# Router products of the values: weights stationary in three column groups, result copied and transposed back

## The chip, the cores and the metric

The kernel runs on one core of a Trainium2 chip. The metric is device time in microseconds (us), the median of three runs. Engines are named as in the profile: PE is TensorE, DVE is VectorE, ACT is ScalarE, POOL is GpSimd, SP is SyncE.

## What is computed

An attention layer with hash buckets (2 batches, 8 heads, 768 tokens, 64 columns a head), a mixture of 8 experts with one expert per token, and a dense layer of two matrices. The change lies in the first two: the router's logits are the attention's output times the gate's weights. The kernel does not form them from the finished output. It multiplies the values with the gate's weights first and lets these products pass through the attention as 8 more columns of each head.

```python
def _attn_ref(q, k, v, proj):
    ...
    mask = q_bucket[:, :, :, None] == k_bucket[:, :, None, :]
    scores = np.where(mask, scale * np.matmul(q, k.transpose(0, 1, 3, 2)), -1000000000.0)
    ...
    return np.matmul(attn, v)

def _moe_ref(x, w_gate, w1, w2, capacity):
    logits = x @ w_gate
    expert_idx = np.argmax(logits, axis=1)
    ...
```

## The kernel before

The order of the work is written out by hand. The attention runs as 96 steps, 16 heads with 6 blocks of keys each (`for k in range(STEPS + LAG + 2)`, line 810). In each step PE gets `scores` of block k (two halves, lines 442 and 443, into two buffers `ps_t`), `mx` of a block 8 steps ahead (two matmuls, line 425, into three buffers `ps_m`), and in every odd step `pv` of two blocks (lines 470 to 472). ACT takes the exponential (444) and makes the high half (452), POOL makes the low half (`plo`, 458), DVE takes the maxima of `mx` (428). Everything else is put on the engines' queues at given moments: `due(x)` (lines 811 and 829) is called at the start of a step (k - 0.5, ahead of `scores`) and at its end (k), and issues whatever `spread` has made due by then; each `yield` of a generator lets d steps pass.

`vgate(r)` (line 522) serves one pair of heads. It is called 8 times; they are called product 0 to product 7 here. Its third part multiplies the pair's values, which lie transposed in `vt` (128 x 768), with the gate's weights `w` (128 x 16: 8 columns for each head of the pair, zero in the other head's rows): six matmuls with 128 columns of `vt` stationary and the 16 columns of `w` moving. The fourth and fifth parts, one for each head, split the result on DVE into a high and a low half in `vh` (lines 540 and 541, called the split here). For products 2 to 7 the parts come one step apart (`vgd`), the third at the start of step 12 r - 2. Product 1 starts at 7.75 (`vg0`), so its third part comes at the end of step 10; product 0 is at steps 2 to 4.

The result lies in `misc`, a pool of a single PSUM bank (`ps_x`, line 312) that six users share in turn. Whoever takes it next can write only when the last reader of the tile before is done. The users that follow a product are `bits` (line 389: `psb`, the projections of four heads, 4 matmuls of 128 x 32 stationary and 384 moving columns into 32 partitions each, two such tiles, then DVE's line 387) and `vscale` (line 558: the maximum `am` on DVE, line 563, is transposed on PE into `psn`, line 571). `vscale(1)` starts at step 13.25 and its transposition stands at the start of step 15; for `vscale(2)` this is the start of step 39, behind product 3; for `vscale(3)` step 63, behind product 5. `bits(2)` comes at the end of step 26, behind product 2, `bits(3)` at the end of step 50, behind product 4.

On DVE's queue there are besides `lo` of a head's preparation (line 375), the low half of the values (line 679) and the maxima of the raw values (line 554).

Of the kernel before, what the change touches and what calls it, by code (L numbers as in the profile page):

```python
# [9 lines left out]
F32 = mybir.dt.float32  # L10
# [9 lines left out]
P = 128  # L20
# [3 lines left out]
NC = S // P  # L24
# [3 lines left out]
KD = DM // P  # L28
E = 8
# [34 lines left out]
def moe_attention_kernel(ctx, tc, qk, v, vt, pj, wg, w1, w2, win, wout, out, cap):  # L64
    nc = tc.nc
    pe, act, dve, pool, sp = nc.tensor, nc.scalar, nc.vector, nc.gpsimd, nc.sync
# [3 lines left out]
    def opened(stack, name, bufs, side="left", **kw):  # L70
        return stack.enter_context(tc.tile_pool(name=name, bufs=bufs, side=side, reuse_waits="tile", **kw))
# [11 lines left out]
    def persist(shape, dt, name):  # L83
        return const.tile(shape, dt, tag=name, name=name)

    xd = dram.tile([NT + 1, DM], F32, tag="xd", name="xd")
    ident = persist([P, P], F32, "ident")
# [6 lines left out]
    iota_s = persist([P, NS], F32, "iota_s")  # L94
    tokid = persist([P, NS], F32, "tokid")
    rank8 = persist([P, E], F32, "rank8")
    wg_sb = persist([P, KD, 2, E], F32, "wg_sb")
    isw = persist([P, 1], F32, "isw")
    lg = persist([P, B, NC, E], F32, "lg")
    ids = persist([P, E, NW], I32, "ids")  # L100
# [84 lines left out]
    def bc(a, n):  # L185
        return a.unsqueeze(len(a.shape)).to_broadcast(list(a.shape) + [n])

    def mid(a, n):
        return a.unsqueeze(1).to_broadcast([a.shape[0], n] + list(a.shape[1:]))
# [114 lines left out]
    with ExitStack() as actx:  # L304
        pa = opened(actx, "pa", 1)
        pr = opened(actx, "pr", 6)
        ph = opened(actx, "ph", 1)
# [35 lines left out]
        def misc(name):  # L343
            return ps_x.tile([P, 512], F32, tag="x", name=name)
# [177 lines left out]
        def vgate(r):  # L522

            sw = sw_t[r // 2]
            t = vt_t.pop(r)
            yield
            yield
            ps = misc(f"psg{r}")
            w = wg_sb[:, r % KD].rearrange("p h e -> p (h e)")
            for j in range(NC):  # L530
                pe.matmul(  # L531
                    ps[:, j * 2 * E : (j + 1) * 2 * E], t[:, j * P : (j + 1) * P], w, start=True, stop=True
                )
            yield
            ps = ps[:, 0 : NC * 2 * E].rearrange("p (c h e) -> p c h e", h=2, e=E)
            for hh in range(2):
                h = 2 * r + hh
                t = vh(h)
                o, ol = hh * D, VA + hh * D
                dve.tensor_scalar(out=t[:, :, o : o + E], in0=ps[:, :, hh], scalar1=sw, scalar2=None, op0=ALU.mult)  # L540
                dve.scalar_tensor_tensor(
                    out=t[:, :, ol : ol + E], in0=ps[:, :, hh], scalar=sw, in1=t[:, :, o : o + E],
                    op0=ALU.mult, op1=ALU.subtract,
                )
                yield
# [68 lines left out]
        def unmatched(r):  # L614

            b, k = divmod(r, KD)
            rows = xd[1 + b * S : 1 + (b + 1) * S, k * P : (k + 1) * P].rearrange("(p c) d -> p c d", c=NC)
            n = 2 * NC * D
            vt = pr.tile([P, S], F32, tag="r", name=f"uv{r}").rearrange("p (h c d) -> p h c d", h=2, c=NC)
            sp.dma_start(out=vt.rearrange("p h c d -> p (h c d)"), in_=v[:, r * n : (r + 1) * n])  # L620
            last = r == NH // 2 - 1
            if not last:
                x = pr.tile([P, S], F32, tag="r", name=f"ux{r}").rearrange("p (c d) -> p c d", c=NC)
                sp.dma_start(out=x, in_=rows)
            m = pt.tile([P, S], F32, tag="pf", name=f"um{r}", bufs=4)
            ps = misc(f"psu{r}")
            for c in range(NC):
                pe.matmul(ps[:, 0:P], ones, vt[:, :, c], start=c == 0, stop=c == NC - 1)
            act.activation(m[:, 0:P], ps[:, 0:P], AF.Copy, scale=1.0 / S)
            ps = misc(f"psc{r}")  # L630
            pe.transpose(ps[:, 0:P], m[:, 0:P], ident)
            act.activation(m[:, P : 2 * P], ps[:, 0:P], AF.Copy, scale=SW)
            ps = misc(f"psl{r}")
            pe.matmul(
                ps[:, 0 : 2 * E], m[:, P : 2 * P], wg_sb[:, k].rearrange("p h e -> p (h e)"), start=True, stop=True
            )
            z = nm[:, 2 * r : 2 * r + 2].rearrange("p h c -> p c h")
            y = pt.tile([P, S], F32, tag="pf", name=f"uy{r}", bufs=4).rearrange("p (c h d) -> p c h d", c=NC, h=2)
            dve.tensor_tensor(
                out=y, in0=bc(z, D), in1=mid(m[:, 0:P].rearrange("p (h d) -> p h d", h=2), NC), op=ALU.mult  # L640
            )
            if last:

                x = xp_t[r][:, :, E : E + D]
                dve.tensor_tensor(out=x, in0=x, in1=y[:, :, 0], op=ALU.add)
                x = pv_t[2 * r + 1][:, 0 : NC * VA].rearrange("p (c d) -> p c d", d=VA)
                t, n = y[:, :, 1], nm[:, 2 * r + 1]
                dve.tensor_scalar(
                    out=t, in0=t, scalar1=sc_t[r // 2][:, 0:1], scalar2=float(S), op0=ALU.mult, op1=ALU.mult
                )  # L650
                dve.tensor_tensor(out=x[:, :, 0:D], in0=x[:, :, 0:D], in1=t, op=ALU.add)
                dve.scalar_tensor_tensor(
                    out=x[:, :, DE], in0=n, scalar=float(S), in1=x[:, :, DE], op0=ALU.mult, op1=ALU.add
                )
            else:
                dve.tensor_tensor(out=x, in0=x, in1=y.rearrange("p c h d -> p c (h d)"), op=ALU.add)
                sp.dma_start(out=rows, in_=x)
            y = pt.tile([P, S], F32, tag="pf", name=f"uz{r}", bufs=4)[:, 0 : NC * 2 * E]
            y = y.rearrange("p (c h e) -> p c h e", c=NC, h=2)
            dve.tensor_tensor(  # L660
                out=y, in0=bc(z, E), in1=mid(ps[:, 0 : 2 * E].rearrange("p (h e) -> p h e", h=2), NC), op=ALU.mult
            )
            for hh in range(2):
                dve.tensor_tensor(out=lg[:, b], in0=lg[:, b], in1=y[:, :, hh], op=ALU.add)

        def vh(h):
            if h not in vh_t:
                vh_t[h] = pt.tile([P, NC, VW], F16, tag="vh", name=f"vh{h}", bufs=4)
            return vh_t[h]
# [34 lines left out]
        for n in range(2):  # L704
            for i, t in enumerate(("X", "K2")):
                c = slice(n * HS, (n + 1) * HS)
                ps = (ps_m, ps_t)[i].tile([P, 512], F32, tag="mt"[i], name=f"psf{n}{i}")
                pe.matmul(
                    ps[D : D + 12, :HS], pj_sb[i * D : (i + 1) * D, 12 * i : 12 * i + 12], r0[i * D : (i + 1) * D, c],
                    start=True, stop=True,  # L710
# [75 lines left out]
        for h in range(NH):  # L786
            k = NC * h + NC - 1 + LAG
            if h < NH - 1:
                at(k + Q["ev"], evac, h)
            if h % 2 == 0:  # L790
                if h == 0:
                    spread(Q["vg0"][0], vgate(0), Q["vg0"][1])
                else:
                    spread(Q["vg0"][2] if h == 2 else NC * h + Q["vg"][h % 4 // 2], vgate(h // 2), Q["vgd"])
            elif h < NH - 1:
                at(k + Q["pa"], pair, h // 2)
                at(NC * h + Q["lvt"], load_vt, h // 2 + 1)
# [35 lines left out]
        with tc.If(ru > 0):  # L833
            for r in range(NH // 2):
                rr = nc.values_load(nflag[0:1, r : r + 1], min_val=0, max_val=2 * S)
                with tc.If(rr > 0):
                    unmatched(r)
            run(route(0, lambda: misc("psr1")))
            run(weigh(0))
        h = NH - 1  # L840
# [633 lines left out]
```

## Time and profile before

| what | us |
|---|---|
| median of three runs | 677.04 (676.58 to 677.83) |
| the profiled execution | 675.88 |
| its span | 674.1 |
| PE busy | 638.4 (95%), 5518 instructions |
| DVE busy | 481.0 (71%), 1038 instructions |
| ACT busy | 426.6 (63%) |
| POOL busy | 229.8 (34%) |

The attention fills the span up to about 235 us, the experts follow to about 410, the dense layer to the end. A matmul's duration includes its way through the array, so matmuls overlap in time; what one adds is read from the distance of two starts. Times of a row are microseconds from the span's start, then the duration; a bracket at the end gives how long the engine stood idle before it and who ended that.

### The profile page before, as it was taken

The page shows a single profiled execution, that of the slowest core. Times are in us where ns is not written, and L with a number is a line of the kernel's source. Part 1 is how long each engine was busy: PE and PEld are TensorE (multiplying, and loading weights), DVE is VectorE, ACT ScalarE, POOL GpSimd, SP SyncE. Part 2 cuts the span into 40 slices and gives each one's busy share as a digit, 9 for nine tenths or more (in the row PEclk, how much of TensorE's full clock was granted, in tenths as well). Part 3 has the DMA queues.
Part 4 walks back from the last instruction along what each step waited for, and adds up shares of the span by engine and source line. Part 5 has one row for each costly group of instructions (what it writes and reads, how often), then busy time and mean ns, then how long its engine had stood idle before and what let it go on. Part 6 is the DMA issues. An engine that isn't in the chain of part 4 may idle for free.

```text
span 674.1 us, 14367 instructions
## 1 busy us (share of the span) xinstructions
PE 638.4 (95%) x5518; PEld 479.7 (71%) x5518; DVE 481.0 (71%) x1038; ACT 426.6 (63%) x869; POOL 229.8 (34%) x199
## 2 busy tenths in 40 slices
PE   7899999999999769999999999999999999999894
PEld 2588889989899638999999997555555555555541
DVE  6768898898999957888888877888888452222320
ACT  3467778778787826776667765455445576555730
POOL 4339769769778233221077500000000021000011
PEclk9889999999999978999999999999999999999998
DMA  8584764764465065777677735443442011000011
GB/s 236 127 233 115 231 177 122 233 169 109 126 160 165 25 217 193 250 246 257 213 253 228 243 115 162 137 145 126 150 134 92 0 48 48 1 0 1 1 41 59
DMA packets 37840, 94.14 MB, mean 140 GB/s; under 512 B 7576, under 2 KB 13720, under 8 KB 37760
## 3 DMA queue, kind: packets, MB, share of 16 engines
q1 hardware_dynamic: 34672, 85.71, 42.7%
q0 software_dynamic: 2400, 7.36, 3.2%
q8 instruction: 46, 0.75, 0.4%
q14 instruction: 34, 0.28, 0.1%
q10 hardware_dynamic: 688, 0.03, 0.1%
HBM read 67.14 MB, written 6.29 MB: 109 GB/s over the span
## 4 chain that ended last, share of the span: by engine, by line
PE 75%; DVE 10%; DMA 6%; ACT 5%; issue 2%; SPq 0%; POOL 0%; POOLq 0%; ACTq 0%; DVEq 0%
PE psg L1249 16%; PE pso L1276 15%; PE psh L1006 11%; PE psy L1033 11%; PE psm L425 5%; PE pst L442 4%; PE pst L443 3%; DVE mx L428 2%; DMA out_dram<-os,inv 2%; PE psv L470 2%; PE psv L471 2%; PE psv L472 2%; PE psg L531 2%; DMA vr<-in_v_dram 1%; ACT junk L1203 1%
## 5 line engine op out<-in xcount | busy, mean ns | idle before, releaser
L458 POOL TENSOR_TENSOR plo<-pf,phi 128x768 f16<-128x768 f32 x86 | 147.1, 1736 | 60.4 <-ACT phi L452 24.9
L444 ACT ACTIVATE pf<-pst 128x384 f32<-128x384 f32 x192 | 83.5, 486 | 47.4 <-PE pst L443 45.7
L428 DVE TENSOR_REDUCE mx<-psm 128x1 f32<-128x384 f32 x192 | 96.3, 548 | 20.0 <-PE psm L425 19.7
L1291 POOL DMA_INDIRECT out_dram<-os,inv x12 | 12.1, 1008 | 270.8 <-DVE os L1283 244.5
L163 DVE SCALAR_TENSOR_TENSOR wl<-raw,wh 128x1024 f16<-128x1024 f32 (+1 forms) x68 | 82.7, 1218 | 6.3 <-ACT wh L157 5.2
L1249 PE MATMUL psg<-yTh,ch 128*128 128x512 f16 (+1 forms) x256 | 83.4, 326 | 3.2 <-DVE rl L1252 3.2
L1249 PE MATMUL psg<-yTl,ch 128*128 128x512 f16 (+1 forms) x256 | 83.4, 326 | 0.0
L1249 PE MATMUL psg<-yTh,cl 128*128 128x512 f16 (+1 forms) x256 | 83.4, 326 | 0.0
L1252 DVE SCALAR_TENSOR_TENSOR rl<-rl,psg 128x512 f32<-128x512 f32 x64 | 35.0, 551 | 64.4 <-ACT rl L1251 64.0
L442 PE MATMUL pst<-Y,K 128*128 128x384 f32 x192 | 75.2, 392 | 2.0 <-ACT pf L444 2.0
L1249 PEld LDWEIGHTS <-ch 128*128 128x128 f16 x512 | 50.0, 98 | 35.9
L452 ACT ACTIVATE phi<-pf 128x768 f16<-128x768 f32 x85 | 71.7, 844 | 1.9
L1276 PE MATMUL pso<-ch,gh 128*128 128x512 f16 x192 | 72.8, 379 | 0.0
L1276 PE MATMUL pso<-ch,gl 128*128 128x512 f16 x192 | 72.8, 379 | 0.0
L1276 PE MATMUL pso<-cl,gh 128*128 128x512 f16 x192 | 72.8, 379 | 0.0
L425 PE MATMUL psm<-K,X 76*128 76x384 f32 x192 | 66.8, 431 | 4.6 <-DVE mx L428 3.8
L157 ACT ACTIVATE wh<-raw 128x1024 f16<-128x1024 f32 (+1 forms) x68 | 67.6, 999 | 0.5 <-issue 0.4
L1276 PEld LDWEIGHTS <-gh 128*128 128x128 f16 x384 | 37.6, 98 | 42.3
L443 PE MATMUL pst<-X,K 77*128 77x384 f32 x192 | 66.5, 346 | 0.0
L1033 PE MATMUL psy<-hh,wl 128*128 128x224 f16 x256 | 66.3, 259 | 0.0
L1033 PE MATMUL psy<-hh,wh 128*128 128x224 f16 x256 | 66.3, 259 | 0.0
L1033 PE MATMUL psy<-hl,wh 128*128 128x224 f16 x256 | 66.3, 259 | 0.0
(231 smaller groups left out, 1495.2 us busy)
## 6 DMA issues: line engine op xcount, KB each, us to landing
raw<-in_w_dram SPq DMA_DIRECT2D x64, 512.0 KB
rc<-in_win_dram SPq DMA_DIRECT2D x16, 512.0 KB
rc<-in_wout_dram SPq DMA_DIRECT2D x16, 512.0 KB
r<-in_qk_dram SPq DMA_DIRECT2D x16, 384.0 KB
K<-hi SPq DMA_DIRECT2D x31, 192.0 KB
vr<-in_v_dram SPq DMA_DIRECT2D x4, 768.0 KB
vt<-in_vt_dram SPq DMA_DIRECT2D x8, 384.0 KB
Y<-hi SPq DMA_DIRECT2D x16, 192.0 KB
```

The source lines that it names most:

```text
L163: dve.scalar_tensor_tensor(out=wl[e, i][:, c : c + n], in0=r, scalar=(S1, S2)[i // 2], in1=wh[e, i][:, c : c + n], op0=ALU.mult, op1=ALU.s ...
L425: pe.matmul(ps[:, :HS], st["X"][0:76, c::NC], st["K2"][0:76, n * HS : (n + 1) * HS], start=True, stop=True)
L428: dve.tensor_reduce(out=mm[:, c, n : n + 1], in_=ps[:, :HS], axis=AX.X, op=ALU.max)
L442: pe.matmul(ps[:, :HS], st["K1"][:, kc], st["Y"][:, qc], start=True, stop=False)
L443: pe.matmul(ps[:, :HS], st["K2"][0:77, kc], st["X"][0:77, qc], start=False, stop=True)
L444: act.activation(pf.rearrange("k (c n p) -> k c n p", c=NC, n=2)[:, :, n], ps[:, :HS].rearrange("k (p c) -> k c p", c=NC), AF.Exp, scale=0 ...
L452: act.activation(phi_t[k], pf_t[k], AF.Copy)
L458: eng.tensor_tensor(out=plo_t[k], in0=pf_t.pop(k), in1=phi_t[k], op=ALU.subtract)
L1006: pe.matmul(ps, l[:, c], r[:, k], start=n == 0, stop=n == 3 * KD - 1)
L1033: pe.matmul(ps, l, r, start=n == 0, stop=n == 3 * KF - 1)
L1249: pe.matmul(ps, l, x, start=n == 0, stop=n == 3 * KD - 1)
L1276: pe.matmul(po[blk][s], l, r, start=first and n == 0, stop=last and n == 2)
```

## The change

The weights get 32 columns (16 of them zeros) and become the stationary side; 256 columns of `vt` move. Three matmuls write 32 partitions each, so the result comes out transposed, 96 x 256, in columns 0 to 255 of the same PSUM tile. DVE copies it to SBUF (`gv`), and two transpositions on PE write it back, token by row, into columns 256 to 447 of the tile, where the split reads it. This makes two parts more: matmuls, copy, transpositions, split of the first head, split of the second head. Nothing else is moved, so both splits come two steps later than before. The clearing and the scaling of `wg_sb`, and its maximum, go over 128 columns where they went over 64.

```diff
-    wg_sb = persist([P, KD, 2, E], F32, "wg_sb")
+    wg_sb = persist([P, KD, 4, E], F32, "wg_sb")
...
             w = wg_sb[:, r % KD].rearrange("p h e -> p (h e)")
-            for j in range(NC):
+            for i in range(3):
                 pe.matmul(
-                    ps[:, j * 2 * E : (j + 1) * 2 * E], t[:, j * P : (j + 1) * P], w, start=True, stop=True
+                    ps[32 * i : 32 * i + 32, 0 : 2 * P], w, t[:, 2 * i * P : (2 * i + 2) * P], start=True, stop=True
                 )
             yield
-            ps = ps[:, 0 : NC * 2 * E].rearrange("p (c h e) -> p c h e", h=2, e=E)
+            gv = ph.tile([96, 2, P], F32, tag="gv", name=f"gv{r}")
+            dve.tensor_copy(gv, ps[0:96, 0 : 2 * P].rearrange("p (m k) -> p m k", m=2))
+            yield
+            ps = ps[:, 2 * P : 2 * P + 192]
+            for m in range(2):
+                pe.transpose(ps.rearrange("p (i m x) -> p m i x", i=3, m=2)[:, m], gv[:, m], ident[0:96, 0:96])
+            yield
+            ps = ps.rearrange("p (c h e) -> p c h e", h=4, e=E)
             for hh in range(2):
...
-                ps[:, 0 : 2 * E], m[:, P : 2 * P], wg_sb[:, k].rearrange("p h e -> p (h e)"), start=True, stop=True
+                ps[:, 0 : 2 * E], m[:, P : 2 * P], wg_sb[:, k, 0:2].rearrange("p h e -> p (h e)"), start=True, stop=True
```

The last edit lies in a branch for rows without a match.

## Rows read from the trace of the kernel before

**Rows 1.** The page: its head, and the chain's shares by engine
```profile
span 674.1 us, 14367 instructions
...
PE 75%; DVE 10%; DMA 6%; ACT 5%; issue 2%; SPq 0%; POOL 0%; POOLq 0%; ACTq 0%; DVEq 0%
```

**Rows 2.** Timeline of PE around product 2 (start, us, engine, line, out<-in)
```profile
76.67 1.48 PE L531 MATMUL psg<-wg_sb,vt 128*128 128x16 f32 x12
78.00 0.42 PE L442 MATMUL pst<-Y,K 128*128 128x384 f32 x1
```

**Rows 3.** Timeline of PE around a tile of bits behind pv
```profile
90.80 0.20 PE L472 MATMUL psv<-vh,plo 128*128 128x73 f16 x1
90.93 0.85 PE L398 MATMUL psb<-r,pj_sb 128*32 128x384 f32 x8
91.71 0.44 PE L442 MATMUL pst<-Y,K 128*128 128x384 f32 x1
```

**Rows 4.** Timeline of PE around four transpositions in the experts
```profile
272.92 0.60 PE L989 MATMUL psa<-ident,xg 128*128 128x128 f32 x4
273.35 0.26 PE L1033 MATMUL psy<-hh,wh 128*128 128x224 f16 x1
```

**Rows 5.** DVE's groups by form: line, op, shapes, count | busy, mean ns
```profile
L1252 DVE SCALAR_TENSOR_TENSOR rl<-rl,psg 128x256 f32<-128x256 f32 x32 | 13.4, 418 | 6.0 <-ACT rl L1251 5.7
```

**Rows 6.** Timeline of all engines where the second tile of bits takes the bank
```profile
50.27 0.85 PE L398 MATMUL psb<-r,pj_sb 128*32 128x384 f32 x8 [0.43 <-DVE b L387]
```

**Rows 7.** Timeline of DVE from step 12 to the maximum that vscale(1) transposes
```profile
57.47 1.02 DVE L428 TENSOR_REDUCE mx<-psm 128x1 f32<-128x384 f32 x2 [0.53 <-PE psm L425]
58.41 1.33 DVE L375 SCALAR_TENSOR_TENSOR lo<-r,hi 128x768 fp32r<-128x768 f32 x1
59.67 0.26 DVE L540 TENSOR_SCALAR vh<-psg,sw 128x48 f16<-128x48 f32 x1
...
60.15 1.01 DVE L428 TENSOR_REDUCE mx<-psm 128x1 f32<-128x384 f32 x2
61.07 0.54 DVE L554 TENSOR_REDUCE am<-vr 128x1 f32<-128x384 f32 x1
61.65 0.16 DVE L563 TENSOR_REDUCE am<-am 128x1 f32<-128x4 f32 x1
```

**Rows 8.** Timeline of PE: the transposition of vscale(1)
```profile
61.86 0.27 PE L571 MATMUL psn<-ident,am 128*1 128x128 f32 x1 [0.43 <-DVE am L563]
```

**Rows 9.** Timeline of DVE: line 375 with POOL idle
```profile
35.10 0.95 DVE L375 SCALAR_TENSOR_TENSOR lo<-r,hi 128x768 fp32r<-128x768 f32 x1
```

**Rows 10.** Timeline of POOL in three stretches
```profile
57.27 1.66 POOL L458 TENSOR_TENSOR plo<-pf,phi 128x768 f16<-128x768 f32 x1
...
84.93 1.65 POOL L458 TENSOR_TENSOR plo<-pf,phi 128x768 f16<-128x768 f32 x1
...
109.67 1.71 POOL L458 TENSOR_TENSOR plo<-pf,phi 128x768 f16<-128x768 f32 x1 [0.23 <-ACT phi L452]
```

**Rows 11.** Timeline of DVE ahead of the transposition of vscale(2)
```profile
111.20 1.00 DVE L375 SCALAR_TENSOR_TENSOR lo<-r,hi 128x768 fp32r<-128x768 f32 x1
...
112.59 1.01 DVE L428 TENSOR_REDUCE mx<-psm 128x1 f32<-128x384 f32 x2
113.52 0.14 DVE L563 TENSOR_REDUCE am<-am 128x1 f32<-128x4 f32 x1
```

**Rows 12.** Timeline of PE: the transposition of vscale(2)
```profile
113.76 0.27 PE L571 MATMUL psn<-ident,am 128*1 128x128 f32 x1
```

**Rows 13.** Timeline of DVE in step 25, behind product 2
```profile
85.83 1.57 DVE L375 SCALAR_TENSOR_TENSOR lo<-r,hi 128x768 fp32r<-128x768 f32 x1
```

**Rows 14.** Timeline of PE: PE waits in step 25, and the first tile of bits(2)
```profile
84.57 0.55 PE L425 MATMUL psm<-K,X 76*128 76x384 f32 x1 [0.33 <-DVE mx L428]
...
87.54 0.85 PE L398 MATMUL psb<-r,pj_sb 128*32 128x384 f32 x8
```

**Rows 15.** Table by stretch: stretch, us, PE busy (x), PEld, DVE, ACT, POOL, granted clock, DMA share, GB/s
```profile
26.83:30.24 3.41, 3.41 (x11) 1.93 (x9) 0.99 (x3) 1.82 (x3) 2.37 (x2) 0.51 1.02 214
```

## The prediction

> **What bounds the kernel now.** I read the page first: PE carries 75% of the chain that ended last, inside a span of 674.1 us [rows 1]. So a microsecond taken from PE in the attention is worth one at the end, as long as PE finds its next operands ready. The second view is PE's timeline around a product: between 40 and 235 us PE issues almost without a gap, and a product is a solid block in it [rows 2]. The third view is PE's few real waits. They are short, and nearly all end with something that DVE has finished: a maximum [rows 14], the maximum that `vscale` transposes [rows 8], the release of the `misc` bank [rows 6]. DVE is therefore the second bound, and the question is what the change puts ahead of those releases. The fourth view is DVE's timeline at these places [rows 7, 11, 13], next to POOL's [rows 10].
>
> **The change part by part.** *The matmuls.* Twelve passes hold PE from 76.67 to 78.00, 1.33 us [rows 2]. The new form stands in the trace with other sizes: four matmuls of 128 x 32 weights and 384 columns into four groups of partitions, eight passes, from 90.93 to 91.71, 0.78 us, 0.13 after the last `pv` matmul where 0.03 is usual [rows 3]. With 256 columns it lies between two thirds of this, 0.52, and all of it, 0.78. I take 0.57, near the lower end, because with 384 columns most of the time is the columns' own. The switch costs 0.10 more. PE saves 1.33 - 0.67 = 0.66 us at each product (0.45 to 0.71).
>
> *The transpositions.* Four of them go from 272.92 to 273.35, 0.11 each [rows 4]; two cost 0.22 (0.06 to 0.55: between passes that overlap wholly and two that follow each other at the 0.27 that one lasts [rows 12]). So PE alone would keep 0.44 at a product.
>
> *The copy.* The trace has no copy of 256 columns out of PSUM. The nearest row is an operation on 128 x 256 that reads PSUM, 0.42 us [rows 5]; the ends are the split's 0.26 for 48 columns [rows 7] and 0.55 for a maximum over 384. I take 0.42. The transposed way needs it ahead of the split, so DVE has 8 x 0.42 = 3.4 us more.
>
> *The order on DVE and the bank.* The split of one head takes DVE 0.48 us, from 59.67 to 60.15 [rows 7]. Both splits now come two steps later, and the bank stays taken until the second is done. The next user of the bank must wait for that, and PE works in order: behind the waiting instruction stand the scores, the maxima's matmuls and `pv`, and so ACT, POOL and DVE. That the bank is waited for is seen in rows 6: `bits` stands 0.43 us because line 387 has not yet read the tile before. In the kernel before, the products' own release was always long past. I go through the places.
>
> *Product 1, then vscale(1).* The matmuls save 0.66, so step 12's maxima start at about 56.8, not 57.47; the row shows that DVE waited 0.53 for PE there. Line 375 follows at 57.7. It takes 0.95 with POOL idle [rows 9] but 1.33 here, and ends at 59.74, 0.81 after POOL's operation of 57.27 + 1.66 = 58.93 [rows 7, 10]; at 84.93 + 1.65 and 109.67 + 1.71 the distance is 0.82 both times [rows 10, 11, 13]. So it waits for POOL's operation and ends at 59.74 again: DVE's lead is gone. After it came the second split, and in its place now only PE's transpositions. Then: maxima 59.67 to 60.60, first split to 61.08, lines 554 and 563 (0.65 from start to the next start) to 61.73, maxima of step 14 to 62.66, second split (0.48 and the 0.06 of its end) to 63.20, and 0.05 for the signal. The transposition of `vscale(1)` starts at 63.25 and not at 61.86 [rows 8]: +1.35 (rounded down; -0.4 if the bank's release hid behind something I overlook, +1.6 if the copy takes 0.55).
>
> *Products 3 and 5, then vscale(2) and vscale(3).* The pattern repeats 52 us later, so one stands for both. Here the splits stood ahead of line 375; now the first stands behind it, between line 554 and the maxima at 112.59, and the second behind line 563 at 113.52 [rows 11]. If line 375 ends at 112.20 as before, the maxima start at 113.07, line 563 at 114.0, the second split ends at 114.6, and the transposition starts at 114.7 where it was at 113.76 [rows 12]: +0.95. DVE reaches line 375 about 1.2 us sooner than at 111.20, near 110.0; POOL's operation began at 109.67 [rows 10], so it is 0.3 too late to pass ahead of it. If it does pass, 1.2 us come back: -0.2. I take +0.95.
>
> *Products 2 and 4, then bits.* The second split now follows line 375, which ends at 87.40 [rows 13], 0.82 after POOL's operation of 84.93 [rows 10]. It ends at 87.9, and `bits`, at 87.54 now [rows 14], starts at 87.95 or so: +0.4. But the splits no longer delay the maxima for which PE waits at 84.57 [rows 14] (0.33 of PE idle, 0.66 with the shortened overlap), and DVE arrives at line 375 at about 84.9, just when POOL's operation starts. If it goes first, nothing waits: -0.44 - 0.66 = -1.1. The ends are too close to call, so I take the middle, -0.4.
>
> *The rest.* Product 0 lies where PE waits for transfers and DVE; the copy lets line 375 at 35.10 [rows 9] start some 0.2 sooner, and the wider clearing, maximum and scaling of the weights cost less than 0.1 (64 columns more, against 0.42 for 256 [rows 5]): -0.2 (-0.4 to +0.3). Product 6: the copy stands behind line 679, which waits for POOL, and the transpositions wait for the copy; between -0.44 (nothing waits) and +0.6: I take +0.2. Product 7 is followed by the stretch without maxima, where DVE and ACT set the pace: 0 (-0.44 to +0.5).
>
> The sum: 1.35 + 2 x 0.95 - 2 x 0.4 - 0.2 + 0.2 + 0 = +2.45 us. Everything behind the attention moves along unchanged. The profiled execution has 675.88 us, its span and 1.8 around it; it would take 678.3. It lies 1.16 below the median of the runs, so the forecast for the median is 677.04 + 2.45 = 679.5 us.
>
> A page speaks to this change. The Trainium skill, page "TensorEngine Tiling (Array Packing)", section "Theoretical Speedup", gives up to four times for a dimension of at most 32; by it the product would take 0.33 and the change would save 8 x (1.33 - 0.33 - 0.22) = 6.2 us. The same page, section "PSUM Bottleneck", says that tiling speeds up TensorE but not the way out of PSUM, whose copy may become the bottleneck; by it the 8 copies of 0.42 would set the time, +3.4 us. Rows 3 show 0.78 us for four groups, which is no fourfold gain for this form, and of the second rule no row shows a case.
>
> **The rivals.** *The covers hold (faster).* If the bank is free when the next user comes, because DVE gets its lines 375 through ahead of POOL everywhere, PE keeps 7 x 0.44 = 3.1 us, and 2 x 0.6 from the wait of rows 14: 677.0 - 4 = 673 us. For it: DVE waits for PE in many places, 0.53 in rows 7. Against it: the second split is the last or the next to last thing on DVE's queue ahead of three transpositions. It decides at 0.4 us of slack per place.
>
> *The fourfold gain.* Three matmuls wholly side by side, at a third or a quarter of 1.33, with no wait for the bank: 671 us. Against it stand the 0.78 of rows 3. It is the case of the page's rule above.
>
> *Gains and waits cancel (no change).* If line 375 passes ahead of POOL at products 2 and 4, or at 3 and 5, but not at both, the sum is 2.45 - 1.4 or 2.45 - 2.3: about 677.1 to 678.1 us. Small shifts of DVE against POOL decide, 0.1 to 0.3 us.
>
> *The clock falls (slower still).* PE would stand still for some 2.4 us ahead of `vscale(1)`. In the first 30 us the granted clock was 0.51, the lower level of 1.2 GHz, from 26.83 on, after PE had stood waiting for DVE [rows 15]. If the long wait does the same here, a stretch like that one, 3.41 us at half speed, costs up to 1.7: 681.2 us.
>
> *The groups don't run side by side (slower; the change would not do what it says).* The eight passes of rows 3 are two rounds of four, 0.39 each; in series six passes at two thirds of that, 0.26, take 1.56: 8 x (1.56 - 0.57) = 8 us more, 687 us. Rows 3 speak against it, as the same call with the same partitions overlaps there.
>
> **How the numbers follow.** Forecast, 679.5 us: 0.52. Covers hold, 673: 0.11. Fourfold gain, 671: 0.02. Cancel, 677.6: 0.25. Clock falls, 681.2: 0.08. No overlap of the groups: 0.02. A measurement of this kernel can tell about 0.2% (1.35 us) from no change. The forecast, the clock and the groups are slower: 0.62. Cancel is the same: 0.25. The rest is faster: 0.13. The forecast's own range is 677.6 (both places of `bits` at -1.1, and 0.5 less elsewhere) to 681.2 (both at +0.4, the copy at 0.55). With the cancelling case and the clock, and part of the case of the covers, the range is 675.8 to 682.0 us.
>
> **What the profile after would show.** The product's matmuls hold PE for 0.6 to 0.7 us, not 1.33; if it is over 1 us, the first step is wrong. The copy lasts 0.38 to 0.45 us whatever POOL does. The transposition of `vscale(1)` shows a wait of PE for the split of about 2.4 us, and those of `vscale(2)` and `vscale(3)` about 1.6; if they start without one, my bank argument fails and the covers held. Line 375 ends 0.8 us after an operation of POOL at these places. At `bits` behind products 2 and 4 there is either a wait of over 1 us, or none and a line 375 of under 1 us. If the waits are as forecast and the total is not, the time came back later, in the waits that I carry over unchanged.

## The result, and the profile after

The changed kernel takes 686.08 us, the median of four runs (685.53 to 686.39), beside 676.81 for the kernel before on the same chip: a ratio of 1.0137, 95% interval 1.0108 to 1.0165, some 9.3 us. A ratio, here and below, leaves out executions over 1.5% longer than the fastest of their kernel: one of x2's ten, three of x9's ten and three of x12's nine. The forecast was 679.5 and its range ended at 682.0. The direction was right, the size was not. The profiled execution takes 685.97 us.

The page's head, its line on the engines and the chain's shares answer [rows 1].

```profile
span 684.3 us, 14313 instructions
PE 639.2 (93%) x5486; PEld 473.6 (69%) x5486; DVE 489.6 (72%) x1046; ACT 427.0 (62%) x869; POOL 231.5 (34%) x199
...
PE 73%; DVE 15%; DMA 5%; ACT 3%; issue 2%; POOL 0%; SPq 0%; DVEq 0%; POOLq 0%; ACTq 0%
```

DVE's share of the chain has gone from 10% to 15%: more of PE's waits end with DVE. The lines behind `vgate` have moved by seven: `am` is transposed on line 578 (571 before), the split stands on 547 and 548 (540 and 541), the low half of the values on 686 (679).

Timeline of PE: a product, the two transpositions, and PE's waits for the bank at vscale(1), bits(2), vscale(2) and bits(3) (start, us, engine, line, out<-in; the bracket is the idle time before and who ended it).

```profile
80.31 0.63 PE L531 MATMUL psg<-vt,wg_sb 128*32 128x256 f32 x6
80.88 0.44 PE L442 MATMUL pst<-Y,K 128*128 128x384 f32 x1
...
56.80 0.33 PE L540 MATMUL psg<-ident,gv 96*128 96x96 f32 x2
56.92 0.42 PE L442 MATMUL pst<-Y,K 128*128 128x384 f32 x1
...
63.30 0.37 PE L578 MATMUL psn<-ident,am 128*1 128x128 f32 x1 [2.45 <-DVE vh L548]
63.33 0.67 PE L442 MATMUL pst<-Y,K 128*128 128x384 f32 x1
...
91.39 0.85 PE L398 MATMUL psb<-r,pj_sb 128*32 128x384 f32 x8 [1.39 <-DVE vh L548]
...
118.54 0.27 PE L578 MATMUL psn<-ident,am 128*1 128x128 f32 x1 [0.46 <-DVE vh L548]
...
144.58 1.34 PE L398 MATMUL psb<-r,pj_sb 128*32 128x384 f32 x8 [1.39 <-DVE vh L548]
```

The product holds PE for 0.57 us instead of 1.33 [rows 2] and the transpositions add 0.12. But five times PE stands still until the second split (548) has released the bank, and at 63.33 and 144.58 the same instructions suddenly take longer: `scores` 0.67 instead of 0.42, `bits` 1.34 instead of 0.85 [rows 14]. The table by stretch says why (stretch, us, busy us of each engine, then the granted clock before the last two columns).

```profile
40.00:62.50 22.50, 20.07 (x248) 16.89 (x244) 20.61 (x42) 16.20 (x29) 14.96 (x9) 1.00 0.72 175
62.50:70.00 7.50, 6.70 (x51) 5.98 (x51) 3.50 (x11) 3.02 (x6) 2.95 (x4) 0.54 0.18 57
70.00:144.50 74.50, 70.20 (x861) 61.99 (x860) 64.48 (x149) 60.23 (x112) 59.49 (x39) 1.00 0.66 186
144.50:148.50 4.00, 3.92 (x27) 2.51 (x28) 2.78 (x8) 1.17 (x3) 3.23 (x3) 0.57 0.83 211
```

Behind these two waits the granted clock is at its lower level of 1.2 GHz. In the kernel before it is 1.00 in every stretch between 41 and 235 us.

DVE in steps 12 to 14 (answering [rows 7]), a copy [rows 5], and line 375 in steps 25 and 38 [rows 13, 11]; then POOL at two of these places [rows 10].

```profile
57.71 2.06 DVE L375 SCALAR_TENSOR_TENSOR lo<-r,hi 128x768 fp32r<-128x768 f32 x1
...
60.63 0.25 DVE L547 TENSOR_SCALAR vh<-psg,sw 128x48 f16<-128x48 f32 x1
...
62.98 0.27 DVE L548 SCALAR_TENSOR_TENSOR vh<-psg,sw,vh 128x48 f16<-128x48 f32 x1
...
83.61 0.41 DVE L536 COPY gv<-psg 96x256 f32<-96x256 f32 x1
...
88.41 2.44 DVE L375 SCALAR_TENSOR_TENSOR lo<-r,hi 128x768 fp32r<-128x768 f32 x1
...
113.78 2.28 DVE L375 SCALAR_TENSOR_TENSOR lo<-r,hi 128x768 fp32r<-128x768 f32 x1
```

```profile
57.30 1.66 POOL L458 TENSOR_TENSOR plo<-pf,phi 128x768 f16<-128x768 f32 x1
...
86.77 3.26 POOL L458 TENSOR_TENSOR plo<-pf,phi 128x768 f16<-128x768 f32 x2
```

Line 375 ends 0.81 us behind POOL's operation of 57.30, as forecast. In step 25 it arrives at 88.41, just as POOL's second operation starts (86.77 and half of 3.26), and so lasts 2.44: it ends 0.82 behind that operation.

How the loss builds up is read from the start of line 442 in each step. The table gives it for all kernels of the next section, as the difference to the kernel before in us. Both times are counted from their span's start. The start of the program differs from execution to execution (step 10: +1.72 to -0.71), so a kernel's column is read from step 10 on. Each line closes one place: vscale(1) at 18, bits(2) at 28, vscale(2) at 40, bits(3) at 54, vscale(3) at 66, product 6 at 78, product 7 at 88.

| step | changed | x1 | x11 | x2 | x12 | x3 | x5 | x13 | x4 |
|---|---|---|---|---|---|---|---|---|---|
| 10 | +0.04 | +0.68 | -0.71 | +0.51 | -0.06 | -0.41 | -0.59 | +1.72 | +0.53 |
| 18 | +4.11 | +1.59 | +2.19 | +0.52 | -0.03 | -0.39 | +1.30 | +3.16 | +1.99 |
| 28 | +3.85 | +1.97 | +2.30 | +0.54 | -0.04 | +1.31 | -0.30 | +2.03 | +2.28 |
| 40 | +4.75 | +2.87 | +3.88 | +0.47 | -0.11 | +2.20 | +2.07 | +2.98 | +3.16 |
| 54 | +6.48 | +3.29 | +2.74 | +0.48 | -0.11 | +3.92 | +1.04 | +1.95 | +4.40 |
| 66 | +7.44 | +4.19 | +5.06 | +0.43 | -0.18 | +4.83 | +3.39 | +2.85 | +6.73 |
| 78 | +9.18 | +5.72 | +6.08 | +0.59 | +0.49 | +6.61 | +4.80 | +4.64 | +9.47 |
| 88 | +10.92 | +7.48 | +8.69 | +2.17 | +0.87 | +9.20 | +6.78 | +7.24 | +11.05 |

The attention of the changed kernel ends 10.9 us later, the profiled execution 10.1 (685.97 against 675.88).

### The profile page after: what moved, and what is told of

It is laid out like the page before. It is cut to its first block, busy times and chain, and to the rows that moved or that the text cites. A ratio compares the mean times of both kernels' runs of the same rounds, so it can differ in the third digit from the quotient of the medians.

```text
span 684.3 us, 14313 instructions
## 1 busy us (share of the span) xinstructions
PE 639.2 (93%) x5486; PEld 473.6 (69%) x5486; DVE 489.6 (72%) x1046; ACT 427.0 (62%) x869; POOL 231.5 (34%) x199
## 4 chain that ended last, share of the span: by engine, by line
PE 73%; DVE 15%; DMA 5%; ACT 3%; issue 2%; POOL 0%; SPq 0%; DVEq 0%; POOLq 0%; ACTq 0%
PE psg L1256 16%; PE pso L1283 15%; PE psy L1040 11%; PE psh L1013 10%; PE psm L425 5%; DVE mx L428 4%; PE pst L442 4%; PE pst L443 3%; DMA out_dram<-os,inv 2%; DVE lo L375 2%; PE psv L470 2%; PE psv L471 2%; PE psv L472 2%; ACT junk L1210 1%; PE psb L398 1%
## 5 line engine op out<-in xcount | busy, mean ns | idle before, releaser
L425 PE MATMUL psm<-K,X 76*128 76x384 f32 x192 | 69.2, 440 | 7.2 <-DVE mx L428 6.3
```

The costliest lines, as they stand in the source:

```text
L425: pe.matmul(ps[:, :HS], st["X"][0:76, c::NC], st["K2"][0:76, n * HS : (n + 1) * HS], start=True, stop=True)
```

## The experiments

**The same order without the new work, x1.** The kernel before with its old products, and only the splits two steps later:

```diff
                     ps[:, j * 2 * E : (j + 1) * 2 * E], t[:, j * P : (j + 1) * P], w, start=True, stop=True
                 )
             yield
+            yield
+            yield
             ps = ps[:, 0 : NC * 2 * E].rearrange("p (c h e) -> p c h e", h=2, e=E)
```

> The kernel before, with its old products, and only the splits two steps later, as the change has them. No copy, no new transposition, no new matmul. Theory (the time is lost because the second split, and with it the release of the misc bank, now stands behind other work on DVE): slower than before by 4 to 7 us; the waits alone give 1.35 at product 1, 0.95 each at products 3 and 5, 0.4 each at products 2 and 4, together 4.05, and up to 3 more if PE's granted clock falls behind the long waits. The transposition of vscale(1) waits about 2 us. Rival (the new matmuls, copies and transpositions cost the time by themselves): within 1 us of before.

Measured: 684.83 us, ratio 1.0139 (1.0104 to 1.0173), the same as the changed kernel within the intervals. Timeline of PE at vscale(1) and bits(2), where the line numbers are two above those of the kernel before:

```profile
63.42 0.27 PE L573 MATMUL psn<-ident,am 128*1 128x128 f32 x1 [1.52 <-DVE vh L543]
...
89.51 0.85 PE L398 MATMUL psb<-r,pj_sb 128*32 128x384 f32 x8 [1.00 <-DVE vh L543]
```

The late release alone, with no copy, no transposition and no new matmul, costs 6.8 us between steps 10 and 88. And the transposition of vscale(1) starts at 63.42 here and at 63.30 in the changed kernel, though PE has some 0.6 us more work here. What sets this moment is POOL, through DVE. Timeline of POOL and of DVE in x1, then of POOL in the changed kernel:

```profile
57.42 1.66 POOL L458 TENSOR_TENSOR plo<-pf,phi 128x768 f16<-128x768 f32 x1 [0.42 <-PE pst L443]
...
58.90 1.00 DVE L375 SCALAR_TENSOR_TENSOR lo<-r,hi 128x768 fp32r<-128x768 f32 x1
```

```profile
50.85 13.63 POOL L458 TENSOR_TENSOR plo<-pf,phi 128x768 f16<-128x768 f32 x8 [5.94 <-DVE phi L454]
```

In both kernels line 375 ends 0.8 us behind POOL's operation (57.42 here, 57.30 there), and the transposition follows 3.5 us later. In the changed kernel this operation is one of a row of eight without a gap, which began at 50.85, before the product's matmuls (52.48), so what these save cannot bring it forward. The saving lengthens PE's wait, from 1.52 to 2.45. At bits(2) the wait is 1.00 against 1.39.

The theory expected 4 to 7 us over the kernel before. The median is 8.4 over (684.83 against 676.40), the profiled execution 6.0. The transposition waits 1.52, where about 2 were expected. This kernel lost 0.9 at vscale(1), not 1.35, and nothing to the clock, which is 1.00 from 40 to 235 us in its profiled execution. That execution, 681.9 us, is the fastest of the four; whether the clock falls in the others, whose mean over the run is 0.976 to 0.979 and not 0.983, no trace shows.

**Less work for PE, x11.** If that reading is right, taking work from PE in x1 must not make it faster:

```diff
-            for j in range(NC):
+            w2 = wg_sb[:, min(r % KD, KD - 2) : min(r % KD, KD - 2) + 2].rearrange("p k h e -> p (k h e)")
+            for j in range(0, NC, 2):
                 pe.matmul(
-                    ps[:, j * 2 * E : (j + 1) * 2 * E], t[:, j * P : (j + 1) * P], w, start=True, stop=True
+                    ps[:, j * 2 * E : (j + 2) * 2 * E], t[:, j * P : (j + 1) * P], w2, start=True, stop=True
                 )
```

> x1 (old products, splits two steps later) with half of each product: three of the six matmuls, each with twice the columns, so that PE has about 0.65 us less at each product, as in the changed kernel, but no copy and no new transposition. Half of the products is left out, so the logits are not those of the reference, and only the attention is compared (start of its last step). Theory (the release of the bank sets the time, PE's saved time only lengthens the wait, and a long wait makes the clock fall): the attention ends no sooner than in x1, 0 to 4 us later, with at least one stretch at the lower clock between 40 and 235 us where x1 has none. Rival (the copy and the transpositions are what the changed kernel pays): the attention ends 3 to 5 us sooner than in x1 and the clock stays full.

Measured: the last steps come 8.7 us later than in the kernel before, 1.2 later than in x1; from step 10 on it loses 9.4 where x1 loses 6.8. (Its whole time, 1854 us, says nothing, since half of each product is left out and the tokens are routed otherwise.) Timeline of PE at vscale(1), and the table by stretch of x11, then of x1:

```profile
62.58 0.27 PE L574 MATMUL psn<-ident,am 128*1 128x128 f32 x1 [2.00 <-DVE vh L544]
...
65.97 0.67 PE L442 MATMUL pst<-Y,K 128*128 128x384 f32 x1
```

```profile
60.00:70.00 10.00, 8.00 (x76) 7.35 (x76) 6.40 (x19) 6.17 (x13) 6.20 (x6) 0.83 0.45 122
...
110.00:165.00 55.00, 53.41 (x621) 47.87 (x619) 45.77 (x107) 44.19 (x82) 44.96 (x31) 0.97 0.62 168
165.00:235.00 70.00, 64.27 (x765) 57.18 (x764) 65.36 (x147) 52.96 (x101) 46.02 (x31) 0.95 0.49 129
```

```profile
60.00:70.00 10.00, 8.48 (x116) 7.84 (x113) 7.78 (x22) 7.62 (x14) 7.36 (x6) 1.00 0.55 152
```

With 0.65 us less to do at each product, PE waits 2.00 instead of 1.52 at vscale(1), and the clock falls there and at three later places. Less work took more time. The rival, by which it should have won 3 to 5 us, is out. But the extra loss comes by way of the clock: its first three falls take 1.5, 1.4 and 1.4 us (steps 15 to 18, 39 to 42 and 63 to 64), while up to step 66 x11 loses only 2.3 more than x1. So this run does not show that PE's saving would be worth nothing at a full clock.

**The release put back, x2.** The changed kernel with products 2 to 7 started two steps earlier, and product 1 with its parts half a step apart (from 8.75), so that the second split stands where it was before:

```diff
+        KEYS = {1: [8.75, 9.25, 9.75, 10.25, 10.75, 11.25, 11.75], 2: [17.5, 18.5, 19.5, 20.5, 21.5, 22.5, 23.5], ...}
...
+                elif h // 2 in KEYS:
+                    g = vgate(h // 2)
+                    for q in KEYS[h // 2]:
+                        at(q, next, g, None)
```

> The changed kernel with the whole product two steps earlier (product 1 in quarter and half steps), so that its second split lands where it was before the change. All the new work stays. Theory (late release): 1 to 4 us below the kernel before, since PE keeps 0.45 to 0.55 us at each of seven products and DVE pays 0.41 at each; no wait ahead of vscale(1) above 0.6 us. Rival (the new work costs it): still 3 us or more over the kernel before.

Measured: 677.70 us, ratio 1.0042 (1.0009 to 1.0074). Neither theory had this: the loss is cut to less than a third, but the gain is not there. Steps 10 to 66 take 0.08 us less than in the kernel before, with the clock at 1.00 throughout. The wait ahead of vscale(1) is 0.56 and ends with `am`, not with the bank. Where PE's half microsecond per product goes shows at product 2: from step 18 to 24 the kernel gains 0.50 and at step 25 it gives 0.51 back. Timeline of POOL and DVE, of x2 and of the kernel before:

```profile
73.70 13.25 POOL L458 TENSOR_TENSOR plo<-pf,phi 128x768 f16<-128x768 f32 x8 [3.93 <-PE psv L472]
...
80.16 1.64 POOL L458 TENSOR_TENSOR plo<-pf,phi 128x768 f16<-128x768 f32 x1
80.17 2.05 DVE L686 SCALAR_TENSOR_TENSOR vh<-vr,sc,vh 128x384 f16<-128x384 f32 x1
```

```profile
73.18 13.41 POOL L458 TENSOR_TENSOR plo<-pf,phi 128x768 f16<-128x768 f32 x8 [3.93 <-PE psv L472]
...
79.61 1.66 POOL L458 TENSOR_TENSOR plo<-pf,phi 128x768 f16<-128x768 f32 x1
80.17 1.52 DVE L679 SCALAR_TENSOR_TENSOR vh<-vr,sc,vh 128x384 f16<-128x384 f32 x1
```

DVE comes to line 686 (679 before) at the same time in both, but ends it 0.53 us later in x2, both times 0.42 behind POOL's operation next to it. POOL's row of eight starts 0.52 later in x2, as that whole execution has run since step 10 (+0.51), and it runs without a gap. So the maxima behind line 686 come no sooner than without the saving, and PE waits for their buffers. At steps 28, 40, 54 and 66 x2's column is back at +0.43 to +0.54 each time. No run moves POOL's operations, so this is read from the rows and not tested.

The other part is lost behind step 66, 1.7 us. There DVE's small operations of the routing stand in another order against POOL's; timeline of DVE in x2, and the same two lines in the kernel before:

```profile
211.04 1.70 DVE L249 SCALAR_TENSOR_TENSOR jt<-tokid,jo 128x24 f32<-128x24 f32 x1
...
216.89 2.24 DVE L458 TENSOR_TENSOR plo<-pf,phi 128x768 f16<-128x768 f32 x1
```

```profile
210.56 0.17 DVE L249 SCALAR_TENSOR_TENSOR jt<-tokid,jo 128x24 f32<-128x24 f32 x1
...
215.39 0.94 DVE L458 TENSOR_TENSOR plo<-pf,phi 128x768 f16<-128x768 f32 x1
```

**Is DVE's copy the rest? x6 and x9.** x6 is x2 with the copy on ACT, x9 is x2 with the copy done twice:

```diff
-            dve.tensor_copy(gv, ps[0:96, 0 : 2 * P].rearrange("p (m k) -> p m k", m=2))
+            act.activation(gv, ps[0:96, 0 : 2 * P].rearrange("p (m k) -> p m k", m=2), AF.Copy)
```

> All products moved two steps earlier as in x2, and the copy done by ACT instead of DVE. Theory (behind the release, what is left of the loss is DVE's work: 8 copies of 0.41 us and the operations that they push into POOL's): the attention ends 2 to 4 us sooner than in x2, so 0.5 to 3 us below the kernel before in all. Rival (what is left is not DVE's load): the same as x2, or later by up to 3 us where ACT's exponentials come late.

> x2 with the copy done twice on DVE, the second one for nothing. It doubles the one cost in question: 8 x 0.41 = 3.3 us more on DVE. Theory (DVE's load sets what x2 lost): 1.5 to 4 us more than x2. Rival (DVE has slack at these places): within 0.7 us of x2.

Measured: 677.87 us, ratio 1.0009 (0.9978 to 1.0040), for x6; 680.29 us, ratio 1.0027 (0.9992 to 1.0063), for x9. Both intervals overlap that of x2: neither removing the copies from DVE nor doubling them moves the time by an amount that can be told. In the profiled execution of x6 the attention loses 3.0 us from step 10 to 88 and in that of x2 1.7; the theory had 2 to 4 less than x2. But 1.5 of x6's loss lies at steps 25 to 27, where its granted clock is 0.57 (84.5 to 88.5 us). The executions of x9 reach from 673.8 to 686.9 us and its profiled one is the longest, so its places are not compared. The theory that DVE's load is what x2 lost is not borne out, and the intervals are too wide to rule it out.

**Products 6 and 7 left alone, x12.** x2 with the old form in the old places for these two:

```diff
+            if r >= 6:
+                w = wg_sb[:, r % KD, 0:2].rearrange("p h e -> p (h e)")
+                for j in range(NC):
+                    pe.matmul(
+                        ps[:, j * 2 * E : (j + 1) * 2 * E], t[:, j * P : (j + 1) * P], w, start=True, stop=True
+                    )
+                yield
+                ps = ps[:, 0 : NC * 2 * E].rearrange("p (c h e) -> p c h e", h=2, e=E)
+            else:
...
```

> x2 with products 6 and 7 in the old form and in their old places; products 1 to 5 in the new form, two steps earlier. Theory (what x2 lost it lost behind step 66, where operations of DVE fell behind POOL's): the attention ends within 1 us of the kernel before and the total is within 1.3 us of it, 1 to 2.5 less than x2. Rival (the new form costs something at each product): as x2.

Measured: the attention ends 0.9 us later than before, as expected, and is level with it at step 66 (-0.18), though products 1 to 5 have the new form: their saving is not kept here either. The total, 680.93 us, is no use as a median (its executions reach from 675.2 to 688.4); the ratio is 1.0039 (0.9996 to 1.0082), unclear, and does not bear out the second half of the expectation. None of the variants tried is shown to be faster than the kernel before.

**One place at a time, x3 and x5.** x3 moves product 1 alone (the key 1 of x2). x5 leaves all in place but puts the second split of products 2 and 4 ahead of line 375 (last key 24.55 and 48.55 instead of 25.5 and 49.5).

> The changed kernel with product 1 alone moved so that its second split lands where it was before the change. Theory (the wait ahead of vscale(1) costs 2.05 us and the fall of the granted clock right behind it another 2.1): about 4 us less than the changed kernel, so about 5 over the kernel before, and no stretch at the lower clock from 63 to 70 us. Rival (the clock falls there for another reason, or its fall costs nothing): at most 2 us less than the changed kernel.

> The changed kernel with one order changed: for products 2 and 4 the second split stands on DVE ahead of line 375 instead of behind it. Theory (line 375, held by POOL, stands between the transpositions and the release of the bank, and the clock falls behind the long wait at bits(3)): the waits of bits(2) and bits(3) go from 1.5 and 1.9 us to under 0.5, and the stretch at the lower clock near 145 us is gone; 3 us less than the changed kernel, about 6 over the kernel before. Rival (the bits wait for something else): waits and time as in the changed kernel.

Measured, x3: 683.74 us, ratio 1.0114 (1.0065 to 1.0163), some 2.3 less than the changed kernel where 4 were expected (the intervals of the two ratios overlap). The place itself did as the theory said: from step 10 to 18 it costs nothing (-0.41 to -0.39; the changed kernel +4.1), and the clock is full there. But it now falls behind the wait at bits(2), where it had not:

```profile
87.44 0.85 PE L398 MATMUL psb<-r,pj_sb 128*32 128x384 f32 x8 [1.38 <-DVE vh L548]
88.22 0.57 PE L442 MATMUL pst<-Y,K 128*128 128x384 f32 x1
```

That wait is the same 1.39 as in the changed kernel. The fall cost 1.4 us there (step 27 to 28).

Measured, x5: 682.96 us, ratio 1.0105 (1.0061 to 1.0150), 3.1 less than the changed kernel; 3 were expected (these intervals overlap too). Both bits start without a wait, where the changed kernel's rows show 1.39 each (the expectation had 1.5 and 1.9):

```profile
87.19 0.85 PE L398 MATMUL psb<-r,pj_sb 128*32 128x384 f32 x8
...
140.45 0.85 PE L398 MATMUL psb<-r,pj_sb 128*32 128x384 f32 x8
```

From step 20 to 28 it gains 1.1 where the changed kernel loses 0.3, and from 42 to 54 it gains 1.0 where that one loses 1.8. Again a part is given back by the clock: it still falls behind vscale(1), after a wait of 1.56, and now also at vscale(2) and vscale(3), 1.4 us each.

**PE kept busy in the waits, x4, x10, x13.** Matmuls of zeros, whose result nobody reads, fill the wait; nothing else changes.

```diff
+        def warm_up(n):
+            heat_t.clear()
+            heat(ps_t, "t", n)
+            heat_t.clear()
+
+        at(14.2, warm_up, 11)
+        at(49.7, warm_up, 9)
```

> The changed kernel with matmuls whose result nobody reads (512 columns; 11 ahead of the transposition of vscale(1), 9 ahead of bits(3)), so that PE works through the two waits behind which the granted clock fell. The waits for the bank stay as they are. Theory (the clock's fall is a price of its own, 2.1 and 0.95 us): 2 to 3 us less than the changed kernel, the granted clock full from 63 to 70 us and from 145 to 148.4. Rival (the clock's fall costs nothing, or does not hang on PE standing still): the same time as the changed kernel, or longer by what the matmuls overrun the waits.

Measured, x4: 685.34 us, ratio 1.0132 (1.0097 to 1.0168), no better than the changed kernel; in the total the rival seems right. The places tell the two apart. The clock is full behind both waits, steps 15 to 18 add 0.03 us (the changed kernel +2.7), steps 51 to 54 add 0.01 (+0.9). But it falls behind the uncovered wait at vscale(3), for 1.4 us, and once more near 205 us. x10 therefore covered all five waits:

> The changed kernel with unread matmuls in all five long waits for the bank (vscale(1) to vscale(3), bits(2), bits(3)), since with two of them covered the clock fell at a third. The waits themselves stay. Theory (the clock's fall behind a long wait is a price of its own): the granted clock is full from 40 to 170 us and the step at 165 us comes 2.5 to 3.5 us sooner than in the changed kernel; in all 2 to 3.5 us less. Rival (the clock falls wherever it likes, or its fall costs nothing): the same as the changed kernel.

Measured, x10: 688.89 us, ratio 1.0179 (1.0119 to 1.0238), a failure for two reasons. At vscale(1) line 375 was held far longer than in any other trace, and the matmuls overran the shorter waits (vscale(2) and vscale(3) cost 1.6 each, 0.9 and 1.0 in the changed kernel). PE then stood 2.47 us for a maximum, ahead of the unread matmuls, and the clock fell there; from 68 to 235 us it is 1.00. So the total says nothing on what the clock's fall costs. Timeline of DVE:

```profile
57.74 4.83 DVE L375 SCALAR_TENSOR_TENSOR lo<-r,hi 128x768 fp32r<-128x768 f32 x1
```

x13 was made with that in mind: x5, in which three waits are left, with fewer matmuls than the waits can hold (7 at 14.2, 2 at 38.2 and 62.2).

> x5 (second split of products 2 and 4 ahead of line 375) with unread matmuls of 512 columns in its three remaining waits for the bank, few enough to end before the waits do: 7 ahead of the transposition of vscale(1), 2 ahead of those of vscale(2) and vscale(3). Theory (the clock's fall is a price of its own): the stretches at the lower clock between 60 and 175 us are gone and it takes 2 to 4 us less than x5. Rival (the fall costs nothing, or has another cause): the same as x5.

Measured, x13: 679.88 us, ratio 1.0047 (1.0029 to 1.0065), 3.1 less than x5. The table by stretch of x13, then of x5:

```profile
60.00:75.00 15.00, 14.20 (x162) 12.02 (x162) 12.60 (x34) 11.29 (x23) 9.70 (x7) 1.00 0.52 138
...
110.00:165.00 55.00, 53.77 (x640) 46.62 (x639) 48.33 (x109) 44.66 (x84) 45.46 (x30) 1.00 0.64 173
165.00:180.00 15.00, 14.04 (x179) 12.29 (x177) 13.58 (x37) 11.40 (x21) 9.37 (x7) 1.00 0.63 163
```

```profile
60.00:75.00 15.00, 13.44 (x149) 12.33 (x148) 11.11 (x33) 10.51 (x20) 7.52 (x6) 0.89 0.53 136
...
110.00:165.00 55.00, 53.42 (x651) 46.75 (x651) 47.62 (x105) 43.32 (x81) 44.03 (x30) 0.97 0.63 172
165.00:180.00 15.00, 13.90 (x149) 12.50 (x149) 12.22 (x37) 10.63 (x20) 8.49 (x6) 0.89 0.55 144
```

From step 10 to 66 x13 loses 1.1 us, x5 4.0. The waits are the same kind; the work added is useless; what is gone is the lower clock. That its fall is a price of its own, about 3 us here, is shown. A part comes back later: by step 88 x13 has lost 5.5 and x5 7.4, and x13's clock falls near 220 us.

## Why the prediction was right in direction and wrong in size

The sum was +2.45 us, the attention measured +10.9. Of the 8.5 us between them, 3.3 lie at products 6 and 7, 3.1 in the clock, which had no term, and 1.9 at bits(2) and bits(3); the rest is 0.2. Step by step:

- **Matmuls, transpositions, copy: right.** 0.57 us for the matmuls (0.57 forecast), 0.12 for the two transpositions (0.22), 0.41 for each of the eight copies (0.42), whatever POOL does.
- **vscale(1): right.** The transposition was forecast at 63.25 and starts at 63.30, with a wait of 2.45 (2.4 forecast); without the clock the place costs 1.4 (1.35).
- **vscale(2) and vscale(3): right in size, +0.90 and +0.96 against +0.95 each.** The wait comes in two pieces, 0.6 for a maximum and 0.46 for the split, and not in one of 1.6. Line 375 came too late to pass POOL, as I had it.
- **bits(2) and bits(3): wrong, +0.3 and +0.8 instead of -0.4 each.** The step that failed is the middle between ends "too close to call". Line 375 either passes or it doesn't, and the middle is a value that cannot occur. At bits(2) it missed by a few hundredths of a us, and the place came out near the forecast's upper end, +0.4. At bits(3) it lies above that end, and why was not taken apart. x5, where the split does not stand behind line 375, shows what such a wait is worth: 1.4 us at bits(2).
- **The clock: mis-placed.** I had it as a rival with a chance of 0.08 and a price of at most 1.7 us, next to a forecast that contained a wait of 2.4 us. It belonged into the sum: 2.1 us net behind vscale(1) (steps 15 to 18 lose 2.7, and 0.55 of it is absorbed by step 20) and 0.95 behind bits(3), 3.1 us in all. x4 and x13 show it.
- **Products 6 and 7: wrong, +1.7 each instead of +0.2 and 0, the largest missing term.** I looked at the copy and at PE's transpositions. But x1, which has neither, loses 1.5 and 1.8 at the same places. The splits, moved two steps back, shift DVE's two-input operations (375, 686, 249, 458) against POOL's. Two of them in the changed kernel (0.93 and 0.17 us in the kernel before):

```profile
200.91 2.06 DVE L686 SCALAR_TENSOR_TENSOR vh<-vr,sc,vh 128x384 f16<-128x384 f32 x1
...
219.83 1.71 DVE L249 SCALAR_TENSOR_TENSOR jt<-tokid,jo 128x24 f32<-128x24 f32 x1
```

  At product 6 most of it is the late split's: x2, with the split back in its place, loses 0.2 there, and x12, with products 6 and 7 as before, 0.7. At product 7 x2 still loses 1.6 and x12 0.4: there the late split alone (x1) or the new form alone (x2) is enough. Which of the shifts counts for how much was not taken apart.
- **What was carried over unchanged: nearly so.** Behind the attention 0.7 us come back in the profiled executions (10.9 there, 10.2 between the spans).

The rival that PE keeps its gain where the bank is free in time was tested by x2: the bank was free, and the gain was still not kept. It was not only the release that set the pace; POOL's row did too, through DVE. So the 0.44 us at a product, from which my sum subtracted, were not to be had in x2's order. My sum knew that lines 375 and 679 wait for POOL, but it counted PE's saving as earned wherever the bank was free, because PE carries 75% of the chain, though PE's next wait for DVE stood three steps behind product 2 [rows 14].

## What to carry to other kernels

A saving on an engine counts only if the next thing it waits for also comes earlier: follow it to that wait before entering it in a sum. If the saved time ends in a wait for another engine, it can cost more than it saves, since a longer wait of PE may bring the lower clock; a wait of over a microsecond in a forecast needs the clock as a term of the sum. Where an operation either passes ahead of another engine's or doesn't, forecast the two cases and not their mean; and if a result in a shared bank must take a detour, put the whole group earlier, so that the release stays where it was.

## What the runs showed of the hardware

The length of a wait alone did not tell whether the clock falls behind it. It fell behind waits of 1.38 to 2.47 us (x3, the changed kernel at bits(3), x5, x11, x10), but also behind 0.65 and 0.46 in short succession (x5, vscale(2)) and in x6 behind 0.26 and 0.38 (steps 24 and 25). It did not fall behind 1.76 (x13, at 51.99), 1.52 (x1) or the 1.39 at bits(2) in the changed kernel. When one fall was taken away, another appeared at a later wait (x3, x4, x5), so no such gain can be counted for one place alone. What sets it is open.

Line 375 can be held by more than one operation of POOL. In x10 it lasted 4.83 us from 57.74, while POOL worked without a gap:

```profile
53.65 8.12 POOL L458 TENSOR_TENSOR plo<-pf,phi 128x768 f16<-128x768 f32 x5
```

It ended 0.80 us behind the last of these. In the changed kernel it got in between two operations that followed each other as closely (88.41 to 90.85, with POOL's second one ending at 90.03). The Trainium skill, page "SBUF — State Buffer", section "Who interferes with whom", says that a DVE instruction with two SBUF inputs contends with a GpSimd instruction that reads SBUF, and that the order of issue decides which of two blocks the other. The trace agrees as far as the first operation goes, the 0.8 us behind POOL's end; that DVE may have to let further ones pass, as in x10, the section doesn't say. When it gets in and when it doesn't is open.
